# A hand-written step plan: batch 1's filter work spread over other steps, batches 2 to 7's inverse units and one chunk moved to neighbouring steps

## The chip, the cores and the metric

The kernel runs on one core of a Trainium2 chip. The metric is the device time of one execution, in microseconds (us). A run reports the median of several executions; one more execution is taken with the hardware profiler, and all lines of profile below are of such an execution.

## What is computed

```python
# x (8, 3008, 256); filt_r, filt_i (1505, 256); w_in (256, 2048); w_out (2048, 256), all float32
X = np.fft.rfft(x, axis=1)
Y = X * (filt_r + 1j * filt_i)[None, :, :]
y = np.fft.irfft(Y, n=3008, axis=1)
h = y.reshape(24064, 256) @ w_in
g = h * np.clip(h + 3.0, 0.0, 6.0) / 6.0
out = g @ w_out
```

A filter along the sequence in the frequency domain, batch by batch, and then an MLP with a hard-swish over all 24064 tokens.

## The kernel before

**The MLP sets the rhythm.** Tokens are handled in 47 blocks of 512 tokens (256 pairs, `PAIRS`). A block takes 8 steps (`NP`), one for each 256 columns of the hidden layer, so the main loop runs over 376 steps. Below, "step 3.1" is step 1 of block 3, that is number 3 * 8 + 1 = 25 of the plan. From block 1 on, both matrix products are done with seven partial products in place of eight. In a step TensorE (PE) makes the seven `up` products of this step (`product`, L764, into the PSUM tiles `al` and `be`) and, between them, the seven `down` products of the step before (`down`, L843, fourteen matmuls from `g` into the four tiles `po`). VectorE (DVE) joins the parts of `h` (L790, L795), multiplies by the clipped gate (`hswish`, L814, twice a step), and makes the sums of `g` that the `down` products read (L821, L822, L827). ScalarE (ACT) copies from PSUM and makes the relu.

The order inside a step is fixed and the same on every engine's queue. What matters here: the first `down` weight load needs the first `hswish`, the next eight `down` weight loads of a step need the second `hswish` (`g_sums`), which stands on DVE's queue behind whatever the last step put at its end.

**The ends of a block.** In step 0 of a block the last `down` of the block before is made, and `out_1` (ACT, L900), `out_2` (DVE, L909) and `out_3` (DVE, L914) take the finished `po` tiles to `o`. In step 1 follow `out_4` (DVE, L918 and L919, and POOL, L920) and `out_5` (DVE, L923). Until L909, L919 and L923 have read their `po` tiles, the `down` products of step 1 that reuse these tiles can't start.

**The filter for the next batch runs in between.** For each batch n from 1 on these pieces of work are laid into the steps:

- `a_unit` / `a6_unit`: first half of the forward transform (PE, L480), stored to `z_tmp`.
- `b_unit`: second half (PE; L548 for batch 1, L539 for later ones), from `t2_load`.
- `f_unit`: the products with the filter (DVE, L560, L561, L562: three operations over 512 columns), with filter rows from `table_load`.
- `y_unit`: the two sums of the complex product (DVE, L571 and L572), into a tile `y` of three buffers.
- `bi3_unit`: first half of the inverse transform for three `y` at a time (PE, L599; DVE L601 and L610, ACT L602 and L609 copy the result), and `g3_store`, four transfers issued on POOL's queue to `g_tmp` (L615, L618). Its PSUM tile `be` is also that of the `up` products.
- `t4_load`: loads from `g_tmp` on SP's queue; `n_five` (five rows at a time, PE, L704, and ACT copies L686) and `n_unit`: second half of the inverse transform, which fills `xn`. When a block's tokens are complete, `t_sums` makes seven sums `xt` on POOL (L760).

Chunk numbers (`n_five(41)`) count the groups of rows over all batches.

**The order is written out by hand.** `at(step, fn, ...)` puts a piece of work into a step. `n_five`, `n_unit`, `a_unit` and `b_unit` go into place 0 of the step, right after the first three `up` products; `bi3_unit` and `a6_unit` into place 1, before the last `up` product; everything else (`f_unit`, `y_unit`, stores and loads) into place 2, at the end of the step. The function `places(n)` gives the steps of a batch: a list for `b_unit` and `f_unit` (twelve entries for batch 1), one for `y_unit`, one for the four `bi3_unit`. `N_AT` and `FIVE_AT` give the steps in which chunks are made, by a letter for the kind of block. For later batches every inverse unit stands at a fixed distance from the batch's first block:

```python
f_at, y_at, bi_at = ([k - (5 - 2 * r) * NP + i for r in range(2) for i in p]
                     for p in ((2, 3, 6, 7, 12, 13), (4, 5, 10, 11, 14, 15), (11, 17)))
```

With `k` the first step of the batch, 17 puts the second and the fourth unit of a batch into step 1 of a block (8.1 and 10.1 for batch 2, 14.1 and 16.1 for batch 3, and so on); 16 is step 0 of the same block.

Of the kernel before, what the change touches and what calls it, by code (L numbers as in the profile page):

```python
# [33 lines left out]
D = 256  # L34
B = 8
# [4 lines left out]
NB = HC // XC  # L40
# [142 lines left out]
def kernel(  # L183
# [794 lines left out]
    with tc.manual_schedule():  # L978
# [127 lines left out]
                kinds[first[n] - 7 + d] = kind  # L1106

        N_AT = {"c": ((6, 6), (3, 3), (6, 6)), "a": ((2, 4), (2, 4), (6, 6)), "A": ((4, 5), (1, 1), (4, 5)), "B": ((2, 3), (1, 1), (2, 3)), "D": ((4, 5), (1, 1), (4, 5))}
        FIVE_AT = {"c": (6, 3, 6), "a": (4, 2, 4), "A": (1, 0, 4), "B": (1, 1, 3), "D": (0, 0, 4)}
        N_FIRST = {0: ((3, 4),), 1: ((), (2, 2), (3, 3)), 2: ((1, 1),), 3: ((1, 1),)}  # L1110
        in_block = {}
        for i in range(2, len(chunks)):
# [2 lines left out]
        for i in range(2, len(chunks)):  # L1115
# [3 lines left out]
            at_, kind = same.index(i) + 1 if len(same) > 1 else 0, kinds.get(k - 1, "a")  # L1119
            steps = N_FIRST[k - 1][at_] if k - 1 in N_FIRST else (FIVE_AT[kind][at_],) * 2 if len(chunks[i][1]) == NJ else N_AT[kind][at_]  # L1120
            if head and len(same) == 1:
# [17 lines left out]

        def places(n):  # L1140
            if n == 1:
                return (list(range(2, NB + 2)), [12, 13, 15, 18, 19, 20, 22, 23, 26, 27, 28, 30],
                        [14, 15, 16, 19, 21, 22, 24, 24, 27, 29, 30, 31], [17, 24, 29, 32])
            k = first[n] * NP
            a_at = [k - 7 * NP + i for i in A_AT]
            f_at, y_at, bi_at = ([k - (5 - 2 * r) * NP + i for r in range(2) for i in p]
                                 for p in ((2, 3, 6, 7, 12, 13), (4, 5, 10, 11, 14, 15), (11, 17)))
            return a_at, f_at, y_at, bi_at

        at(n_at[TAIL - 2] + 1, lambda: nc.sync.dma_start(edge, wai_d[:, ds(NW + ND, ND)]))  # L1150
# [2 lines left out]
        for n in range(1, B):  # L1153
            a_at, f_at, y_at, bi_at = places(n)
            for c, s in enumerate(a_at):
                at(s, a_unit if n == 1 else a6_unit, n, c)
                at(s, a_sums if n == 1 else a6_sums, n, c)
                at(s, *((z_store, n, c, nc.sync) if n == 1 else (z6_store, n, c)))
                if c >= (3 if n == 1 else 2):
                    at(max(a_at[c - 3 + (n > 1)], s - 6), x_load, n, c)  # L1160
                elif n > 1:
                    at(max(prev[-1 if n == 2 else c - 2], s - 6), x_load, n, c)
            for c in range(NT):
                s = f_at[2 * (c - TB) + (n == 1)] + 1 if c >= TB else a_at[-1] + 1
                at(s, t2_load, n, c)
                s = f_at[2 * (c - FB) + 1] + 1 if c >= FB else a_at[-1 if n > 1 else 3] + 1
                at(s, table_load, n, c)
            for i in range(NU):
                if i % 2 == 0 or n == 1:
                    at(f_at[i], b_unit, n, i)  # L1170
                if i % 3 == 0:
                    at(bi_at[i // 3], bi3_unit, n, i)
                    at(bi_at[i // 3], g3_store, n, i)
                at(y_at[i], y_unit, n, i)
            for i in range(NU):
                at(f_at[i], f_unit, n, i)
            prev = a_at
# [9 lines left out]
        for i in range(len(items) + 1):  # L1187
            up = i < len(items)
            k, p = items[min(i, len(items) - 1)]
# [98 lines left out]
```

## Time and profile before

| | |
|---|---|
| three runs, median (lowest to highest) | 2647.28 us (2647.25 to 2647.94) |
| the profiled execution, its own time | 2648.2 us |
| its span in the profile | 2646.4 us |
| PE busy | 2628.5 us, 99% |
| PE weight loads busy | 2338.1 us, 88% |
| DVE busy | 2051.1 us, 78% |
| ACT busy | 1296.5 us, 49% |
| POOL busy | 486.6 us, 18% |
| granted TensorE clock | 1.0 |

Times in the lines of profile count from the start of the span. A step begins where PE loads the weights of its first `up` product (an L764 line `al<-xt`), so the windows view, asked with these moments as bounds, gives a table by step: the first column is the stretch, the second its length, and then come the busy time and the number of instructions of each engine, the granted clock, and the share and rate of the DMA engines. In a timeline line, what stands in brackets is the idle time of the engine before the instruction and what ended it. The profiled execution is some 0.9 us slower than the median of the runs.

### The profile page before, as it was taken

To read this page: it belongs to the slowest core of one execution; us is meant where nothing else is said; L and a number is where in the kernel's file an instruction comes from. 1 tells how busy PE (TensorE), PEld (TensorE's weight loads), DVE (VectorE), ACT (ScalarE), POOL (GpSimd) and SP (SyncE) were. 2 spreads that over 40 slices of the span, in tenths; PEclk is the share of its full clock that TensorE was granted. 3 is DMA by queue.
4 is the path that set the end of the run, shared out by engine and by line. 5 is a ranking of instruction groups with operands and counts; after the bars stand their busy time and mean duration, and the time that the engine had idled before them with its cause. 6 is when DMAs were issued, how large, how long until landed. Compare 5 with 4: busy or idle time off the path is not lost.

```text
span 2646.4 us, 54959 instructions
## 1 busy us (share of the span) xinstructions
PE 2628.5 (99%) x21920; PEld 2338.1 (88%) x21920; DVE 2051.1 (78%) x3611; ACT 1296.5 (49%) x2677; POOL 486.6 (18%) x711
## 2 busy tenths in 40 slices
PE   8999999999999999999999999999999999999999
PEld 6588888989889898898988989889888898999998
DVE  7878867887678876788767887788877888766666
ACT  4554444444544445444454544545445454454554
POOL 2242022111211202111021210211112120111110
PEclk9999999999999999999999999999999999999999
DMA  9732234212241132411233112331123411110000
GB/s 242 222 89 78 70 85 112 59 32 80 78 120 52 32 83 80 116 52 34 83 83 109 53 37 80 89 104 52 51 66 89 104 56 48 48 43 22 19 21 25
DMA packets 130710, 198.29 MB, mean 75 GB/s; under 512 B 21602, under 2 KB 97472, under 8 KB 130262
## 3 DMA queue, kind: packets, MB, share of 16 engines
q1 hardware_dynamic: 115165, 150.12, 20.8%
q0 software_dynamic: 14720, 44.16, 6.0%
q8 instruction: 173, 2.83, 0.4%
q14 instruction: 83, 0.68, 0.1%
q10 hardware_dynamic: 569, 0.50, 0.1%
HBM read 122.43 MB, written 83.98 MB: 78 GB/s over the span
## 4 chain that ended last, share of the span: by engine, by line
PE 97%; DVE 2%; DMA 1%; issue 0%; ACT 0%; SPq 0%; POOL 0%; POOLq 0%; DVEq 0%
PE po L843 43%; PE al L764 24%; PE be L764 18%; PE psn L704 2%; PE psf L539 1%; PE psf L480 1%; PE po L886 1%; PE psf L599 1%; PE be L599 1%; PE be L480 1%; DMA w_all<-in_x_dram 1%; PE al L875 0%; PE be L875 0%; PE po L548 0%; DVE g L814 0%
## 5 line engine op out<-in xcount | busy, mean ns | idle before, releaser
L843 PEld LDWEIGHTS po<-w_all,g 128*128 128x128 f32 x10276 | 1369.6, 191 | 111.7 <-issue 15.5
L843 PE MATMUL po<-w_all,g 128*128 128x128 f32 x10276 | 1394.5, 276 | 3.7 <-DVE g L814 2.4
L809 ACT ACTIVATE r<-h,half_c 128x512 f32<-128x512 f32 x736 | 531.0, 721 | 341.8 <-DVE h L790 329.7
L764 PE MATMUL al<-xt,w_all 128*128 128x256 f32 x2208 | 659.6, 381 | 0.1
L814 DVE SCALAR_TENSOR_TENSOR g<-r,h 128x512 f32<-128x512 f32 x736 | 534.1, 727 | 152.5 <-ACT r L809 136.6
L764 PE MATMUL be<-xt,w_all 128*128 128x256 f32 x1472 | 437.8, 379 | 0.0
L790 DVE TENSOR_TENSOR h<-be,s 128x512 f32<-128x512 f32 x368 | 253.8, 690 | 147.5 <-PE be L764 138.6
L764 PEld LDWEIGHTS al<-xt,w_all 128*128 128x128 f32 x2208 | 335.4, 192 | 1.0 <-issue 0.5
L764 PEld LDWEIGHTS be<-xt,w_all 128*128 128x128 f32 x1472 | 279.7, 190 | 37.9
L760 POOL TENSOR_TENSOR xt<-xn 128x256 f32<-128x256 f32 x184 | 147.9, 822 | 892.9 <-ACT xn L686 858.9
L804 ACT ACTIVATE h<-al 128x256 f32<-128x256 f32 x368 | 141.4, 384 | 291.4 <-PE al L764 291.4
L795 DVE TENSOR_TENSOR h<-al,s 128x256 f32<-128x256 f32 x368 | 156.1, 424 | 153.0 <-PE al L764 146.5
L822 DVE TENSOR_TENSOR g<-g 128x512 f32<-128x512 f32 x367 | 261.3, 712 | 12.6
L785 ACT ACTIVATE s<-al 128x256 f32<-128x256 f32 x368 | 141.4, 384 | 214.4 <-PE al L764 212.9
L764 PE MATMUL al<-xn,w_all 128*128 128x256 f32 x736 | 226.5, 389 | 0.0
L776 ACT ACTIVATE s<-be 128x256 f32<-128x256 f32 x368 | 141.4, 384 | 171.0 <-PE be L764 171.0
L764 PE MATMUL be<-xn,w_all 128*128 128x256 f32 x736 | 218.9, 379 | 0.0
L821 DVE TENSOR_TENSOR g<-g 128x256 f32<-128x256 f32 x367 | 167.4, 456 | 12.6
L775 ACT ACTIVATE s<-al 128x256 f32<-128x256 f32 x368 | 141.1, 383 | 64.6 <-PE al L764 64.6
L827 DVE TENSOR_TENSOR g<-g 128x256 f32<-128x256 f32 x367 | 160.1, 436 | 2.5
L764 PEld LDWEIGHTS be<-xn,w_all 128*128 128x128 f32 x736 | 139.8, 190 | 18.9
L920 POOL TENSOR_TENSOR o<-p,o 128x256 f32<-128x256 f32 x46 | 36.8, 799 | 597.2 <-DVE o L918 551.9
(170 smaller groups left out, 1927.2 us busy)
## 6 DMA issues: line engine op xcount, KB each, us to landing
t<-g_tmp SPq DMA_DIRECT2D x184, 120.0 KB
t<-z_tmp SPq DMA_DIRECT2D x42, 512.0 KB
g_tmp<-t POOLq DMA_DIRECT2D x68, 256.0 KB, 5.7
z_tmp<-t POOLq DMA_DIRECT2D x120, 144.0 KB, 3.5
o_tmp<-o SPq DMA_DIRECT2D x46, 256.0 KB
xs<-in_x_dram SPq DMA_DIRECT2D x60, 192.0 KB
ft<-in_filt_r_dram SPq DMA_DIRECT2D x168, 64.0 KB
ft<-in_filt_i_dram SPq DMA_DIRECT2D x168, 64.0 KB
```

The source lines that it names most:

```text
L760: nc.gpsimd.tensor_tensor(out=o, in0=x0, in1=x1, op=op_)
L764: nc.tensor.matmul(ps, w_in[p][:, w, :], x, start=start, stop=stop, skip_group_check=True)
L776: nc.scalar.activation(out=s5, in_=be[:, 1, :], func=AXT.Copy)
L785: nc.scalar.activation(out=s[:, 1, :], in_=al, func=AXT.Copy)
L790: nc.vector.tensor_tensor(out=st["h"][0].rearrange("p (a n) -> p a n", a=2), in0=be, in1=s, op=ALU.add)
L795: nc.vector.tensor_tensor(out=st["h"][1][:, 256:512], in0=al, in1=s5, op=ALU.add)
L809: nc.scalar.activation(out=r, in_=st["h"][i], func=AXT.Relu, bias=half_c, scale=1.0 / 6.0)
L814: nc.vector.scalar_tensor_tensor(out=st["g", k, p][:, o:o + 2, :].rearrange("p a n -> p (a n)"), in0=st["r", i], scalar=1.0, in1=st["h"][i ...
L821: v.tensor_tensor(out=g[:, G1, :], in0=g[:, G3, :], in1=g[:, G22, :], op=ALU.add)
L822: v.tensor_tensor(out=g[:, G3:G2 + 1:2, :], in0=g[:, G3:G1 + 1, :], in1=g[:, G11:G11 + 1, :].broadcast_to([P, 2, 256]), op=ALU.subtract)
L827: nc.vector.tensor_tensor(out=g[:, G4, :], in0=g[:, G12, :], in1=g[:, G2, :], op=ALU.subtract)
L843: nc.tensor.matmul(st["po", k][bank][:, part, u, :], g[:, a, ts(u, P)], w_out[p][:, w, :], start=(p == 0 and n in OPENS and u == 0), stop= ...
```

## The change

Only numbers in the plan change; every operation, tile and transfer stays, and none is added or taken away.

```diff
-        FIVE_AT = {"c": (6, 3, 6), "a": (4, 2, 4), "A": (1, 0, 4), "B": (1, 1, 3), "D": (0, 0, 4)}
+        FIVE_AT = {"c": (6, 3, 6), "a": (4, 2, 4), "A": (1, 0, 4), "B": (1, 1, 3), "D": (0, 0, 1)}
...
             if n == 1:
-                return (list(range(2, NB + 2)), [12, 13, 15, 18, 19, 20, 22, 23, 26, 27, 28, 30],
-                        [14, 15, 16, 19, 21, 22, 24, 24, 27, 29, 30, 31], [17, 24, 29, 32])
+                return (list(range(2, NB + 2)), [12, 13, 14, 18, 19, 20, 22, 23, 26, 27, 29, 31],
+                        [13, 15, 16, 19, 21, 22, 24, 25, 28, 30, 30, 32], [17, 24, 30, 34])
...
             f_at, y_at, bi_at = ([k - (5 - 2 * r) * NP + i for r in range(2) for i in p]
-                                 for p in ((2, 3, 6, 7, 12, 13), (4, 5, 10, 11, 14, 15), (11, 17)))
+                                 for p in ((2, 3, 6, 7, 12, 13), (4, 5, 10, 11, 14, 15), (11, 16)))
```

What this does to the steps:

- **Batch 1.** `b_unit` and `f_unit` number 2 go from step 1.7 to 1.6, number 10 from 3.4 to 3.5, number 11 from 3.6 to 3.7. `y_unit` number 0 goes from 1.6 to 1.5, number 7 from 3.0 to 3.1, number 8 from 3.3 to 3.4, number 9 from 3.5 to 3.6, number 11 from 3.7 to 4.0. The third `bi3_unit` and its stores go from 3.5 to 3.6, the fourth from 4.0 to 4.2.
- **Batches 2 to 7.** The second and the fourth `bi3_unit` of each batch, with their stores, go from step 1 to step 0 of the same block: twelve units in all. In 8.0, 14.0, 20.0, 26.0, 32.0 and 38.0 a `n_five` stands in the same step.
- **One chunk.** `n_five(41)` goes from step 32.4 to 32.1.

## Prediction, made before the run

> **What bounds the kernel.** I read the page's chain first, then the waits, then the windows view with one window per step, and last the timeline inside the steps that are longer than their work.
>
> ```profile
> span 2646.4 us, 54959 instructions
> ...
> PE 97%; DVE 2%; DMA 1%; issue 0%; ACT 0%; SPq 0%; POOL 0%; POOLq 0%; DVEq 0%
> ```
>
> ```profile
> PEld po L843 <- DVE g L814: 10.5, 13, 1.3
> ...
> PEld po L843 <- DVE o L919: 3.1, 6, 1.5
> ```
>
> PE sets the end; the change adds no PE work, so it can only win or lose what PE waits for. Those waits are few, and DVE ends them.
>
> ```profile
> core 0: us, PE busy (x) PEld busy (x) DVE busy (x) ACT busy (x) POOL busy (x), PEclk, DMA share, GB/s
> 166.32:173.33 7.01, 7.01 (x49) 6.55 (x47) 6.55 (x12) 3.38 (x9) 0.00 (x0) 1.00 0.01 2
> 173.33:179.48 6.15, 6.15 (x45) 5.79 (x44) 5.81 (x11) 3.38 (x9) 0.00 (x0) 1.00 0.31 85
> 186.49:193.85 7.36, 6.44 (x45) 5.73 (x44) 7.01 (x13) 3.58 (x8) 0.00 (x0) 1.00 0.01 2
> 217.27:224.63 7.36, 7.30 (x49) 6.48 (x48) 7.01 (x13) 2.98 (x7) 0.00 (x0) 1.00 0.44 137
> 253.00:262.38 9.38, 8.24 (x125) 6.80 (x124) 8.88 (x16) 4.39 (x10) 7.48 (x10) 1.00 0.34 86
> 313.84:319.99 6.15, 6.15 (x45) 5.79 (x43) 5.19 (x12) 3.36 (x8) 3.04 (x5) 1.00 0.56 145
> 525.78:533.43 7.65, 7.65 (x124) 6.96 (x123) 5.15 (x10) 4.47 (x10) 3.47 (x5) 1.00 0.01 2
> 533.43:541.49 8.06, 8.06 (x69) 6.65 (x68) 6.95 (x14) 3.59 (x8) 3.05 (x4) 1.00 0.14 40
> 640.63:648.49 7.86, 7.86 (x69) 6.72 (x68) 6.19 (x14) 3.58 (x8) 0.72 (x1) 1.00 0.17 46
> 1878.38:1885.36 6.98, 6.42 (x45) 5.71 (x44) 6.60 (x10) 2.98 (x7) 2.76 (x3) 1.00 0.01 2
> ```
>
> These are, in order, steps 1.5, 1.6, 2.0, 2.4, 3.1, 4.1, 8.0, 8.1, 10.1 and 32.5. A bare step is 6.15 us. On it, a `b_unit` of batch 1 costs 0.86 (1.5), `bi3_unit` 1.71 (10.1), `n_five` 1.51 (7.66 - 6.15). What is longer is a stall: 2.0 has no PE extra and yet 1.21 over; 2.4 has one `b_unit` and 0.35 over; 3.1 has `n_five` and 1.72 over; 32.5 is 0.83 over; 8.1 is 0.20 longer than 10.1.
>
> ```profile
> 190.29 0.97 PEld L843 LDWEIGHTS po<-w_all,g 128*128 128x128 f32 x8 [1.32 <-DVE g L814]
> ...
> 260.12 0.97 PEld L843 LDWEIGHTS po<-w_all,g 128*128 128x128 f32 x8 [1.47 <-DVE o L919]
> ```
>
> ```profile
> 1877.14 1.22 DVE L814 SCALAR_TENSOR_TENSOR g<-r,h 128x512 f32<-128x512 f32 x1
> 1878.39 1.10 DVE L571 TENSOR_TENSOR y<-s 64x512 f32<-64x512 f32 x1
> 1879.53 1.10 DVE L572 TENSOR_TENSOR y<-s 64x512 f32<-64x512 f32 x1
> 1880.74 1.03 DVE L814 SCALAR_TENSOR_TENSOR g<-r,h 128x512 f32<-128x512 f32 x1
> ```
>
> The first line is in 2.0: a step that ends with both a `y_unit` and an `f_unit` (1.7) leaves five operations of 0.69 us ahead of the second `hswish`, on which eight weight loads wait. The second is in 3.1: two `y_unit` ahead of the reads that free `po`. The last fence is 32.4 to 32.5: while POOL makes `t_sums`, the same operations, elsewhere 0.69, take 1.03 to 1.22.
>
> **The sum, batch 1.** PE work only moves, so I count stalls.
>
> *Gone.* 2.0 (1.21): 1.7 now ends with one `y_unit`. 3.1 (1.72): one `y_unit` ahead of it, and 2.1, with the same load (`n_five`, one `y_unit` from 2.0), shows no wait for L919 and its L923 6.09 us into the step, in time. 3.4 (0.35): 3.3 ends with an `f_unit` alone. 3.7 (1.21): 3.6 now holds `bi3_unit` and two `y_unit`. From 3.0, where L610 starts 1.19 us before the step's end, its 0.61 and four sums at 0.72 to 0.80 put the second `hswish` 2.4 into 3.7, done at 3.1; it is needed at 2.51 + 0.86 = 3.37, with the `b_unit` as cover. Without that cover 0.6 would stay. Together 4.49.
>
> *New.* 1.6: 1.5 now ends with `y_unit` and `f_unit`, and 1.6 has a `b_unit`: the pattern of 2.4, 0.35. 3.1 itself: 9.1 (`n_five` in step 1, POOL at work) takes 7.70 where 7.66 is its work: 0.04.
> 4.1: a `y_unit` comes from 4.0, and no PE extra covers it. By rows: L914 at +0.31 (4.1), sums at +0.75 and +1.47 (3.1: 253.75, 254.47), `hswish` 0.80 later (2.1: 195.49 to 196.29), done at +2.96; the weight load that stands at +2.51 goes at +3.01, 0.50 late. L919 comes 2.12 after `hswish` (314.49 to 316.61), ends at +4.81; its load stood at +3.83, now 4.33, and goes at 4.86: 0.53 more. Together 1.03.
> 3.2: the `y_unit` that now ends 3.1 runs beside `t_sums`. From L923 at +6.09: L827 0.33 later, `hswish` 0.56 later (3.1), then spacings of 1.25, 1.14 and 1.21 and a last 1.03 (the four lines above): done at +11.61, which is 3.91 into 3.2, needed at 3.37: 0.6 with the hand-over. Nothing if POOL were done by then (spacings of 0.72), 1.0 if all took the longest seen, 1.25; I take 0.6, as 32.5 is the same pattern.
> New together 2.02. Batch 1: -2.47.
>
> The Trainium skill ("SBUF — State Buffer", section "SBUF: two separate sides") speaks against this step: the port pair that VectorE and GpSimd share is locked for a whole instruction, and a VectorE operation with two SBUF inputs waits out a GpSimd operation that reads SBUF. By it each spacing would be 0.69 plus a whole POOL sum of 0.70 (three of them took 2.10 at 529.80) in place of the four lines' mean of 1.16, some 0.9 us more in 3.2, and the whole would be -3.3. The row shows less, so I stay with the row.
>
> **Batches 2 to 7.** Second units: 8.0 and 8.1 are 7.65 + 8.06 = 15.71. Unit and `n_five` in one step have been seen: 2.1 takes 9.39, that is 6.15 + 1.51 + 1.71 and 0.02. So 9.37 + 6.15 = 15.52: -0.19. The 0.20 of 8.1 is a wait for L919 of 0.33 (537.57), with DVE slowed beside `t_sums`; it goes because the unit's 1.71 now lies between. Five times (8, 14, 20, 26, 38): -0.95. In block 32 no `t_sums` runs then and 32.1 is 7.86, so nothing.
> Fourth units: step 4.0 has a unit in step 0 and takes 7.85, 10.1 takes 7.86: zero, six times. What hides them is that L610 (0.69) is done before the next step's `be` product, and that L909 follows at once; without that each costs 0.69 + 0.16.
> `n_five(41)`: 32.5's 0.83 goes, since `y_unit` and `t_sums` no longer meet; in 32.1 it costs 0.04 more as in 9.1, and 32.2 has an `f_unit` that reads PSUM and, like 12.2 after 12.1, no stall (7.37 both). -0.79.
>
> **Transfers.** `bi3_unit`'s four stores (POOL, 0.60 and 0.70 each) start 4.17 after its first matmul (311.01 to 315.18), the last 5.75 after, and land a median 5.7 later. For the fourth unit of batch 1, now in 4.2, that is 16.5 into 4.2, 2.0 into 4.4; `a6_unit` writes that buffer 5.76 into 4.4, so 3.7 of cover. `t4_load` for chunk 8 (SP, issued at 324.18) now waits until 4.4 + 2; behind it stand another `t4_load` and an `x_load` that waited for 4.4 + 6.68 anyway; its reader, `n_five(8)`, is at 4.4 + 15.5. `t2_load` and `table_load` for 1.6 were issued in 1.3 (153.22) and 1.0 (131.13), and the DMA share is 0.01 in 1.5: landed. `table_load` for chunk 2 of batch 1 follows an `f_unit` that ends 1.4 later in 1.6; its reader is 40 us away (218.20). POOL's L920 stands behind the four stores in 8.1 and 10.1 now, as in 4.1, which is bare. So nothing for transfers; if one did wait, about 1 us, once.
>
> **Sum:** -2.47 - 0.95 - 0.79 = -4.21. The profiled execution's span would go from 2646.4 to 2642.2, its own time from 2648.2 to 2644.0. It stands 0.9 over the median of the runs; taken from the median, 2647.28 - 4.21 = 2643.1. No change, within 0.2% (5.3 us, about what a measurement of this kernel can tell), though nearly at that bound.
>
> **Rivals.**
> *The new stalls don't come.* If the sums of 4.1 and 3.2 and the `b_unit` of 1.6 find cover, -4.49 - 0.95 - 0.79 = -6.2: 2641.1, faster. For it: 2.1 covers the same `y_unit`. Against: it does so with 1.51 of `n_five`, which 4.1 lacks. A little over half of the 2.02 is enough to cross the bound. 0.14.
> *Stalls only move.* DVE holds the same work, 7.01 busy in the 7.36 of 2.0. If batch 1 gives all back (3.2 at 1.5, 1.6 and 4.1 longer, a load late), 0 - 1.74: 2645.5. For it: DVE operations beside POOL have taken up to 1.22 for 0.69. Against: bare steps such as 4.2 have 2 us of DVE idle. 0.12.
> *Step 0 is the wrong place.* L601 and L610 stand ahead of L909 and L914, which free `po` for step 1. If those 0.85 us reach PE in all twelve moved units, +10.2, and the 0.95 isn't won: 10.2 - 2.47 - 0.79 = +6.9, 2654.2, slower. It decides from 0.71 us a unit. Against: 3.0 and 4.0 already have units in step 0 and are 7.85, and 4.1 after it is 6.15, with L914 0.31 into the step. 0.07.
>
> **Chances.** My sum 0.67, the rivals 0.14, 0.12 and 0.07. The sum's own error is the 0.6 of 3.2 either way and some 0.3 in each new stall: 2642 to 2644. The range goes on to the first two rivals, 2641.2 to 2645.5. Faster: 0.14 and 0.02 of the sum's tail, 0.16; slower 0.07; within the bound 0.77.
>
> **What the next profile shows.** Right: 2.0, 3.4 and 32.5 at 6.15, 3.1 near 7.70, 3.7 at 7.01; 1.6 at 7.36, 3.2 near 7.6, 4.1 near 7.2; 8.0 at 9.37 and 8.1 at 6.15; 10.0 at 7.86 and 10.1 at 6.15. Wrong: a wait for L909, L914 or L610 in any step 1, or a DMA as a releaser of PE.

## Result and the profile after

| | before | after |
|---|---|---|
| median of 20 runs each (lowest to highest) | 2647.44 us (2645.71 to 2648.77) | 2643.06 us (2642.15 to 2644.23) |
| ratio after to before, 95% interval | | 0.9984 [0.9977, 0.9991] |
| span of the profiled execution | 2646.4 us | 2640.5 us |
| from the start of step 1.0 to the start of step 46.7 | 2502.86 us | 2498.66 us |

The kernel is 4.4 us faster, 0.16%, inside the 0.2% that the prediction called no change and close to its bound; the interval leaves out 1. The forecast was 4.21 us less and 2643.1.

The last row is the one that I compare steps by. The span alone would mislead: it shrank by 5.9, but 1.67 of that lies before step 1.0, which starts at 126.78 in place of 128.45 with the same instructions ahead of it. Between the starts of 1.0 and 46.7 the difference is 4.20.

From the page after, the span and the chain of waits:

```profile
span 2640.5 us, 54927 instructions
...
PE 97%; DMA 1%; DVE 1%; issue 0%; ACT 0%; SPq 0%; POOL 0%; POOLq 0%; DVEq 0%; ACTq 0%
```

From the waits of PE's weight loads after (total, times, longest):

```profile
PEld po L843 <- DVE o L919: 0.6, 1, 0.6
```

DVE's share of the chain went from 2% to 1%. The wait for L919 was met six times before (3.1 and the five steps like 8.1); it is met once after, in 4.1.

The windows after, with the same columns as before: steps 1.6, 2.0, 3.1, 3.2, 4.1, 8.0, 8.1, 10.1 and 32.5.

```profile
171.66:179.01 7.35, 7.29 (x48) 6.48 (x47) 7.00 (x13) 3.34 (x9) 0.00 (x0) 1.00 0.23 63
185.16:191.31 6.15, 6.15 (x45) 5.79 (x44) 5.43 (x10) 3.47 (x8) 0.00 (x0) 1.00 0.01 3
...
250.42:258.14 7.72, 7.72 (x125) 7.03 (x124) 6.93 (x14) 4.44 (x10) 5.83 (x9) 1.00 0.41 105
258.14:265.77 7.63, 7.27 (x48) 6.46 (x47) 7.27 (x11) 2.92 (x7) 3.42 (x4) 1.00 0.16 42
306.96:314.11 7.15, 6.69 (x45) 5.61 (x43) 6.72 (x14) 2.98 (x7) 0.72 (x1) 1.00 0.11 37
521.61:530.98 9.37, 9.37 (x149) 7.90 (x147) 6.24 (x12) 5.08 (x11) 5.10 (x7) 1.00 0.01 2
530.98:537.13 6.15, 6.15 (x45) 5.79 (x44) 5.36 (x12) 3.36 (x8) 3.55 (x6) 1.00 0.55 139
637.98:644.13 6.15, 6.15 (x45) 5.79 (x44) 5.18 (x12) 3.36 (x8) 3.05 (x5) 1.00 0.54 141
1873.52:1879.67 6.15, 6.15 (x45) 5.79 (x44) 5.24 (x10) 2.98 (x7) 0.00 (x0) 1.00 0.02 8
```

2.0, 8.1 and 32.5 are bare steps now, and 3.1 holds only its `n_five`. 1.6, 3.2 and 4.1 took new stalls. 3.2 before, with the same `b_unit` in it:

```profile
262.38:269.39 7.01, 7.01 (x49) 6.55 (x48) 5.90 (x9) 2.97 (x7) 2.28 (x3) 1.00 0.18 49
```

The timeline of DVE after, in 3.1 and 3.2, and then of POOL beside it:

```profile
257.57 1.21 DVE L814 SCALAR_TENSOR_TENSOR g<-r,h 128x512 f32<-128x512 f32 x1
258.81 1.10 DVE L571 TENSOR_TENSOR y<-s 64x512 f32<-64x512 f32 x1
259.94 1.10 DVE L572 TENSOR_TENSOR y<-s 64x512 f32<-64x512 f32 x1
261.15 1.03 DVE L814 SCALAR_TENSOR_TENSOR g<-r,h 128x512 f32<-128x512 f32 x1
```

```profile
258.19 1.18 POOL L760 TENSOR_TENSOR xt<-xn 128x256 f32<-128x256 f32 x1
259.44 1.05 POOL L760 TENSOR_TENSOR xt<-xt 128x256 f32<-128x256 f32 x1
260.46 1.17 POOL L920 TENSOR_TENSOR o<-p,o 128x256 f32<-128x256 f32 x1
```

The last L814 is the second `hswish` of 3.2. It ends at 262.18, 4.04 into the step.

The timeline of 4.1, the two weight loads that PE is late with, and the products of the first:

```profile
310.08 0.97 PEld L843 LDWEIGHTS po<-w_all,g 128*128 128x128 f32 x8 [0.64 <-PE be L764]
310.11 1.13 PE L843 MATMUL po<-w_all,g 128*128 128x128 f32 x8 [0.27 <-DVE g L814]
...
311.87 0.30 PEld L843 LDWEIGHTS po<-w_all,g 128*128 128x128 f32 x2 [0.60 <-DVE o L919]
```

The view puts the wait of the first load down to PE's own `be`, but that product ended at 309.84, before the second `hswish` of this step, which runs from 309.27 to 309.96 and ends 0.12 before the load. The products of that load are put down to it (L814). It is the releaser.

### The profile page after: what moved, and what is told of

Its sections match the earlier page's. It is cut to its first block, busy times and chain, and to the rows that moved or that the text cites. A ratio compares the mean times of both kernels' runs of the same rounds, so it can differ in the third digit from the quotient of the medians.

```text
span 2640.5 us, 54927 instructions
## 1 busy us (share of the span) xinstructions
PE 2626.3 (99%) x21920; PEld 2338.3 (89%) x21920; DVE 2046.7 (78%) x3611; ACT 1296.5 (49%) x2677; POOL 485.5 (18%) x711
## 4 chain that ended last, share of the span: by engine, by line
PE 97%; DMA 1%; DVE 1%; issue 0%; ACT 0%; SPq 0%; POOL 0%; POOLq 0%; DVEq 0%; ACTq 0%
PE po L843 43%; PE al L764 24%; PE be L764 18%; PE psn L704 2%; PE psf L539 1%; PE psf L480 1%; PE po L886 1%; PE psf L599 1%; PE be L599 1%; PE be L480 1%; PE al L875 0%; PE be L875 0%; DMA ft<-in_filt_i_dram 0%; PE psf L453 0%; PE psn L715 0%; DMA wa<-wb_t 0%
## 5 line engine op out<-in xcount | busy, mean ns | idle before, releaser
L814 DVE SCALAR_TENSOR_TENSOR g<-r,h 128x512 f32<-128x512 f32 x736 | 533.9, 727 | 147.6 <-ACT r L809 132.4
L790 DVE TENSOR_TENSOR h<-be,s 128x512 f32<-128x512 f32 x368 | 253.6, 689 | 144.8 <-PE be L764 136.2
L760 POOL TENSOR_TENSOR xt<-xn 128x256 f32<-128x256 f32 x184 | 149.7, 833 | 905.8 <-ACT xn L686 905.8
L764 PEld LDWEIGHTS al<-xn,w_all 128*128 128x128 f32 x736 | 111.4, 191 | 24.7 <-issue 22.3
```

The source lines that it names most:

```text
L760: nc.gpsimd.tensor_tensor(out=o, in0=x0, in1=x1, op=op_)
L764: nc.tensor.matmul(ps, w_in[p][:, w, :], x, start=start, stop=stop, skip_group_check=True)
L790: nc.vector.tensor_tensor(out=st["h"][0].rearrange("p (a n) -> p a n", a=2), in0=be, in1=s, op=ALU.add)
L814: nc.vector.scalar_tensor_tensor(out=st["g", k, p][:, o:o + 2, :].rearrange("p a n -> p (a n)"), in0=st["r", i], scalar=1.0, in1=st["h"][i ...
```

## Experiments

Each kernel was run with a profile, and only the last two in further runs beside it; the times that decide are step lengths, read as above. They can carry this: the changed kernel, profiled a second time, takes 2498.72 from the start of 1.0 to the start of 46.7, 0.06 from the first, and no step between them differs by more than 0.01. Below, "cover" is TensorE work that hides a wait.

### The three parts of the change, each alone

The kernel before with one part of the diff. First the lists of batch 1:

```diff
-                return (list(range(2, NB + 2)), [12, 13, 15, 18, 19, 20, 22, 23, 26, 27, 28, 30],
-                        [14, 15, 16, 19, 21, 22, 24, 24, 27, 29, 30, 31], [17, 24, 29, 32])
+                return (list(range(2, NB + 2)), [12, 13, 14, 18, 19, 20, 22, 23, 26, 27, 29, 31],
+                        [13, 15, 16, 19, 21, 22, 24, 25, 28, 30, 30, 32], [17, 24, 30, 34])
```

> The kernel before with the four lists of batch 1 alone. My theory (stalls taken out and put in, no other cost): 2.0 falls from 7.36 to 6.15, 3.1 from 9.37 to 7.71, 3.4 and 3.7 lose their stalls, 1.6 gains 0.35 beside its b_unit, 3.2 0.63, 4.1 1.00; the steps from 1.0 to 7.7 together are 2.50 us shorter and all later steps are unchanged. Rival (stalls only move): the steps of blocks 1 to 4 together within 0.5 of before, or a load late in blocks 4 to 6 gives it back.

Measured: step 2.0 takes 6.15, 3.1 7.71, 3.4 6.15, 3.7 7.01; 1.6 takes 7.36, 3.2 7.64, 4.1 7.15. From 1.0 to 7.7 the kernel is 2.47 shorter, and no later step differs. The rival, stalls that only move, is out.

The units of batches 2 to 7:

```diff
-for p in ((2, 3, 6, 7, 12, 13), (4, 5, 10, 11, 14, 15), (11, 17)))
+for p in ((2, 3, 6, 7, 12, 13), (4, 5, 10, 11, 14, 15), (11, 16)))
```

> The kernel before with the second and fourth inverse units of batches 2 to 7 in step 0 and nothing else changed. My theory: 8.0 + 8.1 goes from 15.71 to 15.52 (9.37 and 6.15), likewise in 14, 20, 26 and 38; 32.1 is then bare, so block 32 gains nothing; 10.0 and 10.1 swap 6.15 and 7.86 for nothing. Together -0.95. Rival (step 0 is the wrong place): each step 1 after such a unit is up to 0.85 longer than 6.15, with a wait for L909 or L914, up to +10.2 in all.

Measured: 8.0 and 8.1 are 9.37 and 6.15, and the same in blocks 14, 20, 26 and 38; the pairs 10.0 and 10.1 and 32.0 and 32.1 only swap lengths. Together -0.95. No step 1 after a moved unit is longer than 6.15.

The chunk:

```diff
-"D": (0, 0, 4)}
+"D": (0, 0, 1)}
```

> The kernel before with n_five(41) in 32.1 in place of 32.4 and nothing else changed, so that in 32.1 it meets the bi3_unit that still stands there. My theory: 32.4 goes from 7.66 to 6.15, 32.5 from 6.98 to 6.15 since t_sums and y_unit no longer meet, and 32.1 from 7.86 to 9.39 as in 2.1: -0.8 in all. Rival (t_sums slows VectorE wherever it lands): 32.1 or 32.2 takes a stall like the 0.83 and the sum is 0.

Measured: 32.4 6.15, 32.5 6.15, and 32.1, which here holds `bi3_unit` and `n_five`:

```profile
1847.81:1857.17 9.36, 9.36 (x149) 7.89 (x147) 6.92 (x14) 4.59 (x10) 5.10 (x7) 1.00 0.01 3
```

That is the sum of the work with nothing on top, so the 0.83 of 32.5 is gone; from 1.0 to 46.7 the kernel is 0.85 shorter. The three parts alone add up to -2.47 - 0.95 - 0.85 = -4.27 against -4.20 for the whole. They are additive but for 0.07, hardly more than the 0.06 between two profiles of one kernel; 0.05 of it is that `n_five(41)` without the unit beside it makes 32.1 7.70, which is 0.04 more than its work, and with the unit 9.36, where none shows.

### How far step 0 is from being the wrong place

The copy of each inverse unit is made twice, with the same data, in the changed kernel:

```diff
             nc.vector.tensor_copy(out=third[:, 2:512], in_=c[:, 2:512])
+            nc.vector.tensor_copy(out=third[:, 2:512], in_=c[:, 2:512])
```

> The changed kernel with the copy L610 of each bi3_unit made twice (the same data, the same result): 0.69 us more of VectorE ahead of L909 and L914 in each of the twelve moved units. It asks how far the step 0 place is from the wrong place. My theory: in the changed kernel L914 of 10.0 waits 0.21 for TensorE and L919 ends 0.65 before its weight load in 10.1 (0.10 and 0.59 in 8.0 and 8.1), so most of the 0.69 is covered: 10.1 and 8.1 grow by 0 to 0.2 each, at most 2.4 in all; 3.1, which takes more than its work already, grows by up to 0.72 and 3.7 by up to 0.6. Rival (the covers are gone already): each of the twelve steps 1 grows by 0.69, 8.3 in all.

Measured, 3.1, 8.1 and 10.1 of this kernel:

```profile
251.24:259.50 8.26, 7.95 (x124) 6.86 (x123) 7.93 (x15) 4.37 (x10) 6.36 (x10) 1.00 0.39 98
...
532.72:539.00 6.28, 6.28 (x45) 5.62 (x43) 6.00 (x13) 3.35 (x8) 3.52 (x6) 1.00 0.56 143
639.85:646.00 6.15, 6.15 (x45) 5.78 (x44) 5.82 (x13) 3.35 (x8) 3.04 (x5) 1.00 0.55 139
```

The 0.69 costs nothing in the six steps like 10.1 and in 32.1, and 0.13 in the five like 8.1. So step 0 has 0.69 or more of cover in the first and about 0.56 in the second; the rival had all of the 0.85 of L601 and L610 reach PE. What the copy uses up is the time until the next `up` product into `be`: in 8.1 the second L610 ends at 533.12, and the load for that product goes at 533.24, after a wait of 0.21 that the view puts down to PE. By the times it is L610 that it waited for; in 10.1 this load has no such wait, and in neither step does a `down` load wait for L919. Where little cover was left the copy shows nearly whole: 3.1 grows by 0.55, 3.7 by 0.48 (3.2 gives 0.11 back). The whole is 1.5 longer where the rival asked for 8.3.

### Each new stall by itself

`y_unit` number 11 from 4.0 to 4.1:

```diff
-[13, 15, 16, 19, 21, 22, 24, 25, 28, 30, 30, 32]
+[13, 15, 16, 19, 21, 22, 24, 25, 28, 30, 30, 33]
```

> The changed kernel with y_unit number 11 at the end of 4.1 in place of 4.0. My theory: the 1.00 of 4.1 is that y_unit and nothing else; 4.1 goes to 6.15, and 4.2, with a bi3_unit late in the step, stays at 7.86, as 2.0 stays at 6.15 behind a lone y_unit: -1.0. Rival (the stall only moves): 4.2 takes 8.4 to 8.9, or bi3_unit waits for y.

Measured, 4.1 and 4.2:

```profile
307.17:313.32 6.15, 6.15 (x45) 5.79 (x43) 5.52 (x13) 2.98 (x7) 0.73 (x1) 1.00 0.14 46
313.32:321.18 7.86, 7.86 (x69) 6.72 (x68) 5.81 (x11) 3.58 (x8) 0.00 (x0) 1.00 0.11 27
```

4.1 is 1.00 shorter, and nothing comes back in 4.2. The same two operations that cost 1.00 ahead of a bare step in which L914, L918 and L919 run as well cost nothing ahead of 4.2, where these are not. That these three make the difference fits the sum for 4.1; no run isolates it.

`y_unit` number 7 from 3.1 to 3.2, out of POOL's way:

```diff
-[13, 15, 16, 19, 21, 22, 24, 25, 28, 30, 30, 32]
+[13, 15, 16, 19, 21, 22, 24, 26, 28, 30, 30, 32]
```

> The changed kernel with y_unit number 7 at the end of 3.2 in place of 3.1, so that the same two operations run when t_sums is done. My theory (the 0.63 of 3.2 is VectorE and POOL slowing each other): 3.2 goes from 7.64 to 7.01, and 3.3, now behind a y_unit and an f_unit with a b_unit as cover, from 7.01 to 7.36 as 2.4: -0.28. Rival (the two operations are late wherever they stand, POOL or not): the 0.63 comes back in 3.3, sum 0.

Measured: 3.2 7.01, 3.3 7.35, together -0.29. The timeline shows the two operations of the `y_unit` at their full speed again:

```profile
264.28 0.69 DVE L571 TENSOR_TENSOR y<-s 64x512 f32<-64x512 f32 x1
265.00 0.69 DVE L572 TENSOR_TENSOR y<-s 64x512 f32<-64x512 f32 x1
```

What is left is the 0.35 of every `y_unit` and `f_unit` ahead of a `b_unit`.

`y_unit` number 0 from 1.5 to 1.6, so that the same five operations stand ahead of a step without cover:

```diff
-[13, 15, 16, 19, 21, 22, 24, 25, 28, 30, 30, 32]
+[14, 15, 16, 19, 21, 22, 24, 25, 28, 30, 30, 32]
```

> The changed kernel with y_unit number 0 at the end of 1.6 in place of 1.5. Then 1.6 ends with y_unit and f_unit and the step behind it, 1.7, has no TensorE work as cover. My theory (a b_unit covers 0.86 of the 1.21): 1.6 goes from 7.35 to 7.01, 1.7 from 6.15 to 7.36: +0.86. Rival (the pair costs 0.35 wherever it stands): 1.7 at 6.50, sum 0.

Measured: 1.6 7.01, 1.7 7.36, so +0.86. 1.7:

```profile
178.84:186.20 7.36, 6.44 (x45) 5.73 (x44) 6.98 (x13) 2.98 (x7) 0.00 (x0) 1.00 0.15 52
```

The pair of units costs 1.21 in the bare step and 0.35 with a `b_unit` in it; the difference is the 0.86 of the `b_unit`, to the hundredth.

`y_unit` 0 and 1 together in 1.6, `b_unit` and `f_unit` 2 in 1.7:

```diff
-[12, 13, 14, 18, 19, 20, 22, 23, 26, 27, 29, 31],
-[13, 15, 16, 19, 21, 22, 24, 25, 28, 30, 30, 32]
+[12, 13, 15, 18, 19, 20, 22, 23, 26, 27, 29, 31],
+[14, 14, 16, 19, 21, 22, 24, 25, 28, 30, 30, 32]
```

> The changed kernel with y_unit 0 and 1 both at the end of 1.6, b_unit and f_unit number 2 back in 1.7, and y_unit 2 in 2.0 as it was. Four VectorE operations then stand ahead of 1.7's second hswish in place of five ahead of 1.6's. My theory (by 3.6 and 3.7 of the changed kernel, where two y_unit ahead of a b_unit cost nothing): 1.6 is 6.15, 1.7 is 7.01, 2.0 is 6.15 and 2.1 stays 9.39: -0.35. Rival (the stall only moves): 1.7 at 7.36 or 2.1 longer, sum 0.

Measured: 1.6 6.15, 1.7 7.01, 2.0 and 2.1 unchanged: -0.34. Four operations of 0.69 ahead of the second `hswish` fit under a `b_unit`, five don't.

### A plan without the new stalls

The findings put together, in the changed kernel. The two kernels were timed side by side with the kernel before; first the changed kernel itself.

> The changed kernel itself, timed beside the one that follows. By the sum 4.2 us under the kernel before, 0.9984 of it.

Measured: median 2642.52 us (2641.60 to 2643.50), 0.9982 [0.9973, 0.9991] of before.

```diff
-[12, 13, 14, 18, 19, 20, 22, 23, 26, 27, 29, 31],
-[13, 15, 16, 19, 21, 22, 24, 25, 28, 30, 30, 32], [17, 24, 30, 34]
+[12, 13, 15, 18, 19, 21, 22, 23, 26, 28, 29, 31],
+[14, 14, 16, 20, 20, 22, 24, 27, 27, 30, 30, 33], [17, 24, 30, 34]
```

> The changed kernel with the lists of batch 1 laid out so that its new stalls go: y_unit 0 and 1 in 1.6 and b_unit 2 in 1.7; y_unit 3 and 4 in 2.4; y_unit 7 and 8 in 3.3; b_unit and f_unit 9 in 3.4; y_unit 11 in 4.1. My theory, step by step against the changed kernel: 1.6 and 1.7 together -0.35, 2.4 -0.35 with 2.5, 3.2 -0.63, 4.1 -1.00, nothing new: 2.33 us less, 6.5 us under the kernel before, 0.9975 of it; 2.7 keeps its 0.35. Rival (VectorE has no room, stalls only move): within 0.5 us of the changed kernel.

Measured: median 2640.44 us (2639.95 to 2642.40), 0.9977 [0.9967, 0.9986] of before, 6.7 us under its median of 2647.14. Against the changed kernel it is 2.1 us less by the medians of the same call, though the two intervals overlap, and 2.3 by the steps (2498.66 to 2496.40 from 1.0 to 46.7). Three of its steps, 2.4, 3.2 and 4.1, and a line of its waits:

```profile
214.42:220.57 6.15, 6.15 (x45) 5.79 (x44) 5.81 (x11) 2.98 (x7) 0.00 (x0) 1.00 0.45 141
...
257.52:264.53 7.01, 7.01 (x49) 6.55 (x48) 6.31 (x9) 2.92 (x7) 3.15 (x4) 1.00 0.17 45
...
305.72:311.87 6.15, 6.15 (x45) 5.79 (x44) 5.53 (x13) 2.98 (x7) 0.73 (x1) 1.00 0.13 43
```

```profile
PEld po L843 <- DVE g L814: 6.3, 8, 0.8
```

PE is busy for all of each of these steps. Before, there were 13 such waits for `hswish`, the longest 1.3; now there are 8 of at most 0.8. The rival, that VectorE has no room, is out: with the same 2047 us of VectorE work as in the changed kernel, the stalls are gone.

## Why the prediction was right

Step lengths, predicted against measured in the changed kernel:

| step | predicted | measured | experiment that isolates it |
|---|---|---|---|
| 2.0, 3.4 | 6.15 | 6.15 | lists of batch 1 alone |
| 3.7 | 7.01 | 7.01 | the same |
| 3.1 | 7.70 | 7.71 | the same |
| 1.6 | 7.36 | 7.35 | `y_unit` 0 later; 0 and 1 together |
| 3.2 | near 7.6 | 7.64 | `y_unit` 7 later |
| 4.1 | near 7.2 | 7.15 | `y_unit` 11 later |
| 8.0, 8.1 | 9.37, 6.15 | 9.37, 6.15 | units alone; copy made twice |
| 10.0, 10.1 | 7.86, 6.15 | 7.86, 6.15 | the same |
| 32.5 | 6.15 | 6.15 | chunk alone |

**Batch 1.** Predicted -2.47, measured -2.49. The stalls gone are those named. The three new ones came where they were put: 0.34, 0.63 and 1.00 for 0.35, 0.6 and 1.03.

**The term with the widest bounds, 3.2.** It was worked out from four lines of 32.4, with spacings of 1.25, 1.14 and 1.21 and a last 1.03. In 3.2 the spacings are 1.24, 1.13 and 1.21, and the last operation takes 1.03. That POOL is the cause is shown by the `y_unit` put behind `t_sums`: 0.69 each, and the 0.63 gone.

The Trainium skill ("SBUF — State Buffer", section "SBUF: two separate sides") says that whichever of a VectorE operation with two SBUF inputs and a GpSimd operation that reads SBUF comes first holds the shared ports for the whole instruction and the other blocks. I had weighed it as 0.9 more in 3.2, 1.5 in all. The trace has 0.63. Both engines are slowed, but a VectorE operation and a POOL operation together take some 1.2 us, less than the 0.69 + 0.70 of the two alone, and the records overlap (258.81 to 259.91 on DVE, 258.19 to 259.37 on POOL). So neither waits out the whole record of the other; whether one of them is shut out for a shorter part of it these records can't show. The measurement decides; the row was the right price.

**4.1.** The two parts of the 1.03 came near what was worked out: the weight load behind the second `hswish` goes 3.12 into the step (predicted 3.01), and that behind L919 4.91 in (predicted 4.86). The step lost 1.00.

**Batches 2 to 7.** Predicted -0.95 for the second units, nothing for the fourth and -0.79 for `n_five(41)`. Measured -0.19 five times, no difference in the six fourth units, and -0.78 in block 32. The reason given for the 0.19 holds too. `t_sums` starts 4.0 into 8.0 in both kernels, but its last sum ends 2.40 into 8.1 before (535.83) and 0.48 into it after (531.46), since 8.0 is longer by the unit. The cover that the prediction named first (L610 done before the next `be`) is there, and its size is now known: 0.56 us where `t_sums` runs in the unit's own step, 0.69 or more where not. 3.7, where the prediction put the second `hswish` 0.27 ahead of its need, had 0.21 by the copy made twice (0.69 less the 0.48 it grew by).

**Rivals.** That the new stalls would not come is refuted by 1.6, 3.2 and 4.1, and it takes another plan to be rid of them. That plan comes near the price of this rival (2641.1 forecast, 2640.4 measured), but it also takes out the 0.35 of 2.4. That stalls only move is refuted by the experiments of batch 1: each stall taken out was gone, and what came elsewhere came where it was expected (0.34 in 3.3 with `y_unit` 7, 1.21 in 1.7 with `y_unit` 0). That step 0 is the wrong place is refuted, with 0.56 us or more of cover to spare in each unit.

**Signs.** Of the two signs of being wrong, the first didn't come: no step 1 waits for L909, L914 or L610. The second, a DMA as a releaser of PE, tells nothing here. The view names one ahead of ten L539 weight loads of the main loop, 0.33 each, and ahead of eight before; the steps that hold the ten have the same length in both profiles. `t4_load` waits 10.8 for the later stores, as foreseen, and no step is longer for it.

**What was not foreseen.** The forecast of the profiled execution, a span of 2642.2, missed by 1.7. The step sum was right to a hundredth (4.21 for 4.20), closer than its own terms, which missed by up to 0.03 and partly cancel; the start of step 1.0 differed, which no step of the sum had as a term. The median of 20 runs, 2643.06, lies within 0.1 of the forecast 2643.1. So close a hit is luck: the runs of one kernel spread over 2 to 3 us, and against the 20 runs of before the fall is 4.38.

## What to carry to other kernels

Where a repeating loop has a bare step of fixed length, price a change of order in stalls per step: count what stands on the slow engine's queue ahead of the operation that the bound engine waits for, and subtract what cover the bound engine has in that step. Here two `y_unit` (four operations) fit under one `b_unit`, a `y_unit` and an `f_unit` (five) cost 0.35, and without the `b_unit` 1.21. When a change moves the whole by less than the runs scatter, compare step lengths of two profiles, not their spans.

## What the runs showed of the hardware

**The scatter sits at the ends.** Over the twelve profiles of this case, from before to the last plan, step 1.0 starts between 126.01 and 128.45 us, though no instruction ahead of it was changed in any, and the last step, 46.7 with what follows it, takes 15.06 to 15.57. Between them a step that a change doesn't touch is the same to 0.04 us in every profile. So the 2 to 3 us between the lowest and the highest run of one kernel can come from what lies ahead of 1.0 and behind 46.7 alone; that they do in the runs without a profile was not shown, nor what makes the start differ. Part of it may be loads: ahead of 1.0 PE waits 2.0 for `w_all<-in_x_dram` in the profile before, 0.3 in the one after.

**VectorE beside POOL.** Where 3.1 meets 3.2 the two share, neither at full speed: DVE operations of 0.69 with both inputs in SBUF take 1.03 to 1.21, POOL's of 0.70 or 0.72 take 1.05 to 1.18. The DVE operation L790, with one input in PSUM, is not slowed: in 3.1 of the changed kernel, in the midst of POOL's first three sums (254.45 to 256.56), it takes the 0.68 that it takes elsewhere. Nor is it in the rest of the loop: the 60 L790 that run beside POOL's sums (L760, L920) for over 80% of their time take 0.69 in the mean, as do the 296 that meet none of its sums; of L814, both inputs in SBUF, 65 run beside them and take 1.08 in the mean (0.68 to 1.22) where 0.69 is usual. From the timeline:

```profile
255.14 0.68 DVE L790 TENSOR_TENSOR h<-be,s 128x512 f32<-128x512 f32 x1
```
